# Output stage of a recurrent attention and maxout FFN kernel: x blocks taken into the Strassen products, and the first group's outputs in the same form

## The chip, the cores and the metric

One core of one Trainium2 chip. The metric is the device time of one execution in microseconds (us). Engines: TensorE (PE, with its weight loads as PEld), VectorE (DVE), ScalarE (ACT), GpSimd (POOL), and SyncE (SP), which here only issues DMAs.

## What is computed

```
batch, n_heads, seq, head_dim = 4, 8, 768, 48          # attention, float32
f = 1 / (1 + exp(-f_logit))
for t in range(seq):
    state = f[t][:, None] * state + outer(k[t], v[t])  # per batch and head, 48 x 48
    y[t] = q[t] @ state
x = y as (3072 tokens, 384)                            # 8 heads of 48 side by side
h = max(x @ w1, x @ w2, x @ w3)                        # 384 -> 768
out = h @ w_out                                        # 768 -> 384
```

## The kernel before

**Units and groups.** The recurrence is computed in chunks of 64 tokens. A unit `u` is one chunk of two batches (128 token rows); there are 24. Four units make a group of 512 tokens (`GRP`, `TOK`), so there are six groups. The attention of a unit is spread over the names `sigmoids`, `scan`, `after`, `before` (gates, keys `kh`, queries `qh`), `keys` and `keys_by_blocks` (keys turned back), `pairs` (line 392, with the causal mask on VectorE in line 395), `values` (lines 411 and 436), `carry` and `finish` (line 500).

**The FFN.** The maxout is taken as `x @ w1 + max(0, x @ (w2 - w1), x @ (w3 - w1))`. The linear part is folded into the output: `out = hm @ w_out + x @ (w1 @ w_out)`, with `hm` the maximum of 0 and the two differences. `linear` (line 745) makes `w1 @ w_out` once: `w_nat` has its rows in natural order, `w_lin` in the order in which later groups hold x (a copy by DMA, `place`). Group 0 has a form of its own, `ffn_first`; groups 1 to 5 make `hm` with `inputs_by_pairs` (line 836), itself a Strassen form, and the outputs with `outputs_by_pairs` (line 609).

**The output stage.** For groups 1 to 5 `hm @ w_out` is done as Strassen-Winograd: the 2x2 blocks are tiles of tokens (n), even and odd blocks of `hm` (k) and halves of the output columns. Seven products, each of three k blocks (`HJ`), 192 columns (`HD`) and two pairs of token tiles (p); `into(bank, p, lhs, rhs)` issues the three matmuls of one product and one pair. The sums of `hm` (s1, s2, s4, and one written in place) come from `sums_of_hm` on GpSimd, called in the last step `fourth(n)` of each third of `hm` after VectorE's two maximum operations (lines 886 and 887). The mixes of `w_out` come once from `mix` on GpSimd. The part `x @ (w1 @ w_out)` is four more products of three x blocks each, so a group takes 66 matmuls of 192 columns. They add into three PSUM banks a, b and c. Bank a is read three times on the way by ScalarE (`read`, line 614) and added to further after each read; VectorE and GpSimd form the output blocks from what was read (lines 617 and 662). In the last group the second half of c lies in b (`d`). Group 0's outputs are plain: `outputs` (line 563) takes, for each of four token tiles, six `hm` blocks and three x blocks of 384 columns: 36 matmuls.

**Order.** The whole kernel stands under a manual schedule: each engine and each DMA queue runs its instructions in the order of the program text. The FFN is a generator that yields the TensorE time of each step, counted as columns times 1.667 ns; the attention loop calls `fill(ns)`, which draws steps until the budget is used up. There are five draws per unit, of `EARLY` ns in units 4 to 7 (the last of the five 1000 less) and of `PART` ns afterwards; before unit 4 there are eight draws of 12,800 ns in all. So a step's place beside the attention follows from the sum of the draws and the sum of the yields. The FFN of a group runs while the units of the next group are computed; group 5's runs alone at the end, beside a check of the weights' range (`check_range`, ScalarE).

Of the kernel before, what the change touches and what calls it, by code (L numbers as in the profile page):

```python
# [9 lines left out]
FP32 = mybir.dt.float32  # L10
# [45 lines left out]
def kernel(  # L56
# [33 lines left out]
    def fast():  # L90
        ctx = ExitStack()
        with ctx:
# [434 lines left out]
            def bank(in_tr=False):  # L527
                if in_tr:
                    return ps_tr.tile([128, TOK], FP32, name="tr")
                return ps_f.tile([128, TOK], FP32, name="p")  # L530
# [26 lines left out]
            def outputs(hm, xT, i):  # L557
                p = bank()
                t = slice(i % 2 * UT, (i % 2 + 1) * UT)
                terms = [(hm[:, j, i * UT:(i + 1) * UT], w_out[:, j, :]) for j in range(NJ)]  # L560
                terms += [(by_halves(xT)[:, i // 2, k, t], w_nat[:, k, :]) for k in range(NK)]
                for n, (lhsT, rhs) in enumerate(terms):
                    nc.tensor.matmul(p[:, 0:DM], lhsT=lhsT, rhs=rhs, start=(n == 0), stop=(n == NJ + NK - 1))  # L563
                    if n % NK == NK - 1:
                        if n == NJ + NK - 1:
                            o = o_four[:, i]
                            nc.scalar.copy(o, p[:, 0:DM])
                            store(i, o)
                        yield NK * DM * COLUMN

            HJ, HD = NJ // 2, DM // 2
            corner = lambda k, n: w_out[:, k::2, n * HD:(n + 1) * HD]
            w_mix = [keep.tile([128, HJ, HD], FP32, name="mix")] + [w_in[2][:, :, n * HD:(n + 1) * HD] for n in range(4)]
            s_mix = [w_in[1][:, n, :].rearrange("q (jj t) -> q jj t", jj=HJ) for n in range(NK)]
            partial = [w_in[0][:, n, 0:DM] for n in range(NK)]
            pairs_of = lambda t: t.rearrange("q (p c) -> q p c", p=2)  # L580

            def mix(n):

                dst, x, y = ((w_mix[2], corner(1, 1), corner(0, 1)), (w_mix[0], corner(0, 1), corner(0, 0)),
                             (w_mix[1], corner(1, 1), w_mix[0]), (w_mix[3], corner(1, 0), w_mix[1]),
                             (w_mix[4], w_lin[:, :, 0:HD], w_lin[:, :, HD:]))[n]
                nc.gpsimd.tensor_tensor(dst, x, y, op=ALU.subtract)

            def sums_of_hm(hm, jj):

                first, second = ([hm[:, 2 * jj + k].rearrange("q (p n t) -> q n p t", p=2, n=2)[:, n] for n in range(2)]
                                 for k in range(2))
                s1, s2, s4 = (pairs_of(t[:, jj]) for t in s_mix)
                for dst, x, y, op in ((s1, first[1], second[1], ALU.add), (s2, s1, first[0], ALU.subtract),
                                      (first[1], first[0], first[1], ALU.subtract), (s4, second[0], s2, ALU.subtract)):
                    nc.gpsimd.tensor_tensor(dst, x, y, op=op)  # L596

            def outputs_by_pairs(g, hm, xT):
                tile_of = lambda p, n: slice((2 * p + n) * UT, (2 * p + n + 1) * UT)
                A = lambda k, n: lambda p: hm[:, k::2, tile_of(p, n)]  # L600
                X = lambda n: lambda p: xT[:, 0:NK, tile_of(p, n)]
                s1, s2, s4 = (lambda p, t=t: t[:, :, p * UT:(p + 1) * UT] for t in s_mix)
                lin = [w_lin[:, :, n * HD:(n + 1) * HD] for n in range(2)]
# [3 lines left out]
                def into(b, p, lhs, rhs):  # L607
                    for k in range(HJ):
                        nc.tensor.matmul(b[:, p * HD:(p + 1) * HD], lhsT=lhs(p)[:, k], rhs=rhs[:, k],  # L609
                                         start=id(b) not in begun, stop=(k == HJ - 1), skip_group_check=True)  # L610
                        begun.add(id(b))

                def read(b, n):
                    nc.scalar.copy(partial[n], b[:, 0:DM])  # L614
# [4 lines left out]
                COST = HJ * HD * COLUMN  # L619
                a, b, c = bank(), bank(True), bank(True)  # L620
                into(b, 0, X(0), lin[0])
                yield COST
                into(b, 1, X(0), lin[0])
                yield COST
                into(a, 0, A(0, 0), corner(0, 0))
                yield COST
                into(b, 0, A(1, 0), corner(1, 0))
                yield COST
                into(a, 1, A(0, 0), corner(0, 0))
                read(a, 0)  # L630
                yield COST
                into(b, 1, A(1, 0), corner(1, 0))
# [4 lines left out]
                into(a, 0, s2, w_mix[1])  # L637
                yield COST
                into(a, 1, s2, w_mix[1])
                read(a, 1)  # L640
                yield COST
                d = b if last else c
                into(c, 0, s1, w_mix[0])
# [4 lines left out]
                into(d, 1, s1, w_mix[0])  # L648
# [5 lines left out]
                into(a, 0, A(0, 1), w_mix[2])  # L654
                yield COST
                into(a, 1, A(0, 1), w_mix[2])
                yield COST
                into(a, 0, X(1), lin[1])
                yield COST
# [3 lines left out]
                if last:  # L663
                    store_part(g, 1, 1)
                yield COST
                into(c, 0, X(0), lin[1])
                yield COST
                into(d, 1, X(0), lin[1])
                yield COST
                into(a, 0, A(1, 1), w_mix[3])  # L670
                yield COST
                into(a, 1, A(1, 1), w_mix[3])
# [3 lines left out]
                into(a, 0, X(1), w_mix[4])  # L676
                yield COST
                into(a, 1, X(1), w_mix[4])
# [3 lines left out]
                yield COST  # L682
                into(c, 0, s4, corner(1, 1))
# [3 lines left out]
                into(d, 1, s4, corner(1, 1))  # L687
# [67 lines left out]
            def ffn_first(xT):  # L755
# [18 lines left out]
                for a in range(NK):  # L774
                    if a < 2:
                        for n in range(2 * NK + 2):
                            place(placed[a].bitcast(FP32), w_in[a + 1], n)
                    for cost in linear(a):
                        round_to(rounded[0] + 1)
                        yield cost  # L780
                for n in range(2 * NK + 2):
                    place(w_lin, w_nat, n)
                made = iter([lambda n=n: mix_in(n) for n in range(4)] + [lambda n=n: mix(n) for n in range(5)])
                for i in range(GRP):
                    for n, cost in enumerate(outputs(hm, xT, i)):
                        if i or n:
                            next(made, lambda: None)()
                        if i == GRP - 1 and n == 1 and 1 in packed:
                            sums_of_x(1)
                        yield cost  # L790
# [33 lines left out]
            def inputs_by_pairs(g, hm, xT):  # L824
# [57 lines left out]
                def fourth(n):  # L882
                    into(A[n], n, w_two[1][:, 1], t4)
                    yield COST
                    into(A[n], n, w_two[1][:, 2], t5)
                    nc.vector.scalar_tensor_tensor(out(n, 0), out(n, 0), 0.0, two(A[n]), op0=ALU.max, op1=ALU.max)
                    nc.vector.scalar_tensor_tensor(out(n, 1), out(n, 1), 0.0, u3, op0=ALU.max, op1=ALU.max)  # L887
                    sums_of_hm(hm, n)
                    yield COST
# [48 lines left out]
            EARLY = 2360  # L938
            PART = (33 * TOK + 22 * HJ * HD) * COLUMN / (5 * GRP)
# [408 lines left out]
```

## Time and profile before

| | us |
|---|---|
| median of 3 runs (423.09 to 423.75) | 423.5 |
| the profiled execution | 423.43 |
| its span, first to last instruction | 421.7 |
| group 0's outputs (98.3 to 127.1) | 28.7 |
| groups 1, 2 and 3, from one group's first FFN product to the next group's | 60.5 each |
| group 5's FFN to the last instruction (366.1 to 421.7) | 55.6 |

Times inside the profile count from the start of the span. A line of the timeline or of the chain has its start, its duration, the engine and the source line, and how many records were merged into it (`x6`); in brackets stands the idle time in front of it and what ended that. A matmul in float32 leaves two MATMUL and two weight load records. "p" and "tr" are the names of the PSUM tiles: bank a is a "p", banks b and c are "tr".

### The profile page before, as it was taken

The page shows a single profiled execution, that of the slowest core. Times are in us where ns is not written, and L with a number is a line of the kernel's source. Part 1 is how long each engine was busy: PE and PEld are TensorE (multiplying, and loading weights), DVE is VectorE, ACT ScalarE, POOL GpSimd, SP SyncE. Part 2 cuts the span into 40 slices and gives each one's busy share as a digit, 9 for nine tenths or more (in the row PEclk, how much of TensorE's full clock was granted, in tenths as well). Part 3 has the DMA queues.
Part 4 walks back from the last instruction along what each step waited for, and adds up shares of the span by engine and source line. Part 5 has one row for each costly group of instructions (what it writes and reads, how often), then busy time and mean ns, then how long its engine had stood idle before and what let it go on. Part 6 is the DMA issues. An engine that isn't in the chain of part 4 may idle for free.

```text
span 421.7 us, 11556 instructions
## 1 busy us (share of the span) xinstructions
PE 402.8 (96%) x4650; PEld 338.5 (80%) x4650; DVE 264.5 (63%) x515; ACT 180.2 (43%) x414; POOL 235.2 (56%) x262
## 2 busy tenths in 40 slices
PE   4978899899999999999999999999999999999995
PEld 3756765466668888998889988889988889988994
DVE  6986594843597699868789867889764730002300
ACT  2478676632114442425531444442254524576210
POOL 2189554621988676376586357576556960435600
PEclk9999999999999999999999999999999999999998
DMA  8999897782547654277645276635473010542002
GB/s 169 232 266 284 236 258 112 121 170 67 102 85 129 87 116 66 60 106 101 117 104 95 56 113 87 144 79 89 64 144 91 11 54 9 158 140 75 2 19 60
DMA packets 175129, 47.20 MB, mean 112 GB/s; under 512 B 154016, under 2 KB 172768, under 8 KB 175072
## 3 DMA queue, kind: packets, MB, share of 16 engines
q1 hardware_dynamic: 171600, 45.61, 52.0%
q10 hardware_dynamic: 3472, 0.81, 0.9%
q8 instruction: 37, 0.61, 0.6%
q14 instruction: 20, 0.16, 0.1%
HBM read 37.75 MB, written 4.72 MB: 101 GB/s over the span
## 4 chain that ended last, share of the span: by engine, by line
PE 86%; SPq 5%; DVE 3%; POOL 2%; issue 1%; ACT 1%; DMA 1%; DVEq 0%; POOLq 0%
PE p L836 19%; PE tr L836 16%; PE p L609 15%; PE tr L609 12%; PE p L563 6%; PE p L537 5%; PE p L745 3%; PE y L500 3%; PE y L411 3%; SPq L164 2%; PE a L392 2%; SPq L174 2%; PE y L436 2%; POOL w_in L258 1%; DMA placed<-in_moe_w_dram 1%
## 5 line engine op out<-in xcount | busy, mean ns | idle before, releaser
L836 PE MATMUL tr<-xT,placed 128*128 128x256 f32 x300 | 73.3, 385 | 0.0
L382 DVE STREAM_TRANSPOSE ks<-kh 32x128 f32<-32x128 f32 x224 | 67.7, 302 | 4.6 <-POOL kh L340 1.0
L836 PEld LDWEIGHTS tr<-xT,placed 128*128 128x128 f32 x300 | 55.6, 190 | 9.1 <-ACT hm L844 1.4
L836 PE MATMUL p<-xT,placed 128*128 128x256 f32 x180 | 45.0, 381 | 0.0
L537 PE MATMUL p<-xT,w_in 128*128 128x256 f32 (+1 forms) x108 | 34.4, 459 | 4.9 <-DVE hm L767 2.2
L836 PEld LDWEIGHTS p<-xT,placed 128*128 128x128 f32 x180 | 33.8, 190 | 4.7
L329 DVE TENSOR_TENSOR_SCAN r<-gate,from_one 128x520 f32<-128x520 f32 x24 | 31.3, 1306 | 8.9 <-ACT gate L308 5.9
L617 DVE TENSOR_TENSOR o<-tr,w_in 128x384 f32<-128x384 f32 (+1 forms) x11 | 5.7, 515 | 48.8 <-PE tr L609 43.5
L340 POOL TENSOR_TENSOR kh<-kt,r 128x512 f32<-128x512 f32 x16 | 28.7, 1796 | 10.6 <-DVE kt L296 10.6
L596 POOL TENSOR_TENSOR w_in<-hm 128x256 f32<-128x256 f32 x15 | 10.9, 727 | 40.5 <-DVE hm L887 40.5
L854 POOL TENSOR_TENSOR hm<-hm,rest_bits 128x512 f32<-128x512 f32 x15 | 22.7, 1514 | 19.2 <-ACT hm L844 19.2
L506 ACT COPY xT<-y 64x256 f32<-64x256 f32 (+1 forms) x60 | 22.1, 369 | 24.1 <-PE y L500 23.4
L347 DVE TENSOR_TENSOR_SCAN prod<-gate,from_inv 128x520 f32<-128x520 f32 x24 | 31.9, 1329 | 0.0
L395 DVE TENSOR_TENSOR at<-a,mask 128x512 f32<-128x512 f32 x24 | 16.5, 688 | 24.2 <-PE a L392 23.9
L836 PE MATMUL p<-w_in,placed 128*128 128x256 f32 x120 | 30.0, 379 | 0.0
L537 PEld LDWEIGHTS p<-xT,w_in 128*128 128x128 f32 x108 | 19.3, 190 | 13.0 <-issue 6.2
L258 POOL TENSOR_TENSOR w_in<-top_bits,rest_bits 128x384 uint32<-128x384 uint32 x18 | 21.8, 1218 | 13.5 <-DVE top_bits L254 8.0
L879 DVE TENSOR_TENSOR hm<-tr,hm 128x512 f32<-128x512 f32 x15 | 10.2, 681 | 29.3 <-PE tr L836 19.3
L662 POOL TENSOR_TENSOR o<-top_bits,w_in 128x384 f32<-128x384 f32 x5 | 5.1, 1018 | 41.6 <-ACT w_in L614 41.6
L614 ACT COPY w_in<-p 128x384 f32<-128x384 f32 x15 | 7.2, 480 | 47.3 <-PE p L609 47.3
L280 ACT ACTIVATE raw<-top_bits 128x384 f32<-128x384 f32 x48 | 25.3, 526 | 0.4
L836 PEld LDWEIGHTS p<-w_in,placed 128*128 128x128 f32 x120 | 22.8, 190 | 3.1
(155 smaller groups left out, 888.4 us busy)
## 6 DMA issues: line engine op xcount, KB each, us to landing
raw<-in_moe_w_dram SPq DMA_DIRECT2D x24, 384.0 KB, 4.2
v_ld<-in_v_dram SPq DMA_DIRECT2D x48, 96.0 KB, 3.3
placed<-in_moe_w_dram SPq DMA_DIRECT2D x12, 384.0 KB, 5.7
out_dram<-o SPq DMA_DIRECT2D x46, 96.0 KB, 2.2
placed<-in_moe_w_out_dram SPq DMA_DIRECT2D x6, 384.0 KB, 5.9
raw<-in_moe_w_out_dram SPq DMA_DIRECT2D x6, 384.0 KB, 3.3
f_ld<-in_f_logit_dram SPq DMA_DIRECT2D x32, 64.0 KB, 2.6
k_ld<-in_k_dram SPq DMA_DIRECT2D x32, 64.0 KB, 2.5
```

The lines of the kernel that those rows point to most:

```text
L258: nc.gpsimd.tensor_tensor(dst, by(top), by(rest), op=ALU.add)
L280: nc.scalar.activation(over, size, AF.Relu, scale=(-1 / HI_MIN, 1.0)[step - 1], bias=(1.0, -HI_END * (1 - 2.0 ** -24))[step - 1], accum_ou ...
L329: nc.vector.tensor_tensor_scan(r[:, 0:LEN][:, ::-1], flat(gate)[:, ::-1], flat(from_one)[:, ::-1], 1.0, op0=ALU.mult, op1=ALU.max)
L340: (nc.vector if u < BY_ROWS else nc.gpsimd).tensor_tensor(kh.rearrange("p h a t -> p a h t"), kt, by_batch(r[:, 1:LEN + 1].rearrange("p (x ...
L347: nc.vector.tensor_tensor_scan(flat(prod), flat(gate_tiles[u % 2]), flat(from_inv[u % 2]), 1.0, op0=ALU.mult, op1=ALU.max)
L382: nc.vector.transpose(ks[n * 32:(n + 1) * 32, :, par, e0:e0 + 32], kh[p0:p0 + 32, :, a, t0:t0 + 32])
L506: nc.scalar.copy(xT[o, :, t0 + a * C:t0 + (a + 1) * C], y[i, a, 0:HP * C].rearrange("p (h t) -> p h t", h=HP))
L537: nc.tensor.matmul(p if w < TOK else p.rearrange("p (two t) -> p two t", two=2), lhsT=w_in[i][:, kt, j * 128:(j + 1) * 128], rhs=x[:, t.st ...
L563: nc.tensor.matmul(p[:, 0:DM], lhsT=lhsT, rhs=rhs, start=(n == 0), stop=(n == NJ + NK - 1))
L609: nc.tensor.matmul(b[:, p * HD:(p + 1) * HD], lhsT=lhs(p)[:, k], rhs=rhs[:, k], start=id(b) not in begun, stop=(k == HJ - 1), skip_group_c ...
L836: nc.tensor.matmul(b[:, j * HALF:(j + 1) * HALF], lhsT=w[:, (2 * n + j) * 128:(2 * n + j + 1) * 128], rhs=x, start=begin and j == 0, stop= ...
L854: nc.gpsimd.tensor_tensor(out(n, 0), out(n, 0), first, op=ALU.add)
```

## The change

Groups 1 to 5: the x blocks 0 and 1 with the matching rows of `w_lin` become a fourth k block of the seven Strassen products (`mixed`), and only x block 2 stays in the four plain products. A group then takes 7·4·2 + 4·1·2 = 64 matmuls of 192 columns. The sums of x come from `sums_of_pair` on VectorE, two of the four operations in `fourth(1)` and two in `fourth(2)`; the mixes of `w_lin` come once, in group 1, from `mix_x` on VectorE.

Group 0 takes `outputs_by_pairs` too, without the mixed block: 66 matmuls of 192 columns. Its `hm` sums come from GpSimd during `linear`, and `mix` moves from GpSimd to VectorE, all five ahead of the first product.

In the order of the products, the s1 products come before the s2 products. `EARLY` goes from 2360 to 2270, and `PART` from 2464 to 2432 by its formula.

```
-            def outputs(hm, xT, i):
...
-            w_mix = [keep.tile([128, HJ, HD], FP32, name="mix")] + [w_in[2][:, :, n * HD:(n + 1) * HD] for n in range(4)]
+            w_mix = [corner(0, 1)] + [w_in[2][:, :, n * HD:(n + 1) * HD] for n in range(4)]
+            x_mix = [w_lin[:, 0, HD:]] + [w_mix[4][:, n] for n in range(2)] + [keep.tile([128, HD], FP32, name="mix")]
...
             def mix(n):
...
-                             (w_mix[4], w_lin[:, :, 0:HD], w_lin[:, :, HD:]))[n]
-                nc.gpsimd.tensor_tensor(dst, x, y, op=ALU.subtract)
+                             (w_mix[4], w_nat[:, :, 0:HD], w_nat[:, :, HD:]))[n]
+                nc.vector.tensor_tensor(dst, x, y, op=ALU.subtract)
+
+            def mix_x(n):
+                of = lambda k, c: w_lin[:, k, c * HD:(c + 1) * HD]
+                dst, x, y = ((x_mix[2], of(1, 1), of(0, 1)), (x_mix[0], of(0, 1), of(0, 0)),
+                             (x_mix[1], of(1, 1), x_mix[0]), (x_mix[3], of(1, 0), x_mix[1]),
+                             (w_mix[4][:, 2], of(2, 0), of(2, 1)))[n]
+                nc.vector.tensor_tensor(dst, x, y, op=ALU.subtract)
+
+            def sums_of_pair(x0, x1, *sums, part=slice(0, 4), engine=nc.gpsimd):
+                first, second = ([x.rearrange("q (p n t) -> q n p t", p=2, n=2)[:, n] for n in range(2)] for x in (x0, x1))
+                s1, s2, s4 = (pairs_of(t) for t in sums)
+                for dst, x, y, op in ((s1, first[1], second[1], ALU.add), (s2, s1, first[0], ALU.subtract),
+                                      (first[1], first[0], first[1], ALU.subtract), (s4, second[0], s2, ALU.subtract))[part]:
+                    engine.tensor_tensor(dst, x, y, op=op)
...
+                A = lambda k, n: lambda p: [hm[:, 2 * jj + k, tile_of(p, n)] for jj in range(HJ)] + [xT[:, k, tile_of(p, n)]] * mixed
...
+                if mixed:
+                    X = lambda n: lambda p: [xT[:, 2, tile_of(p, n)]]
...
+                    X = lambda n: lambda p: [by_halves(xT)[:, p, k, n * UT:(n + 1) * UT] for k in range(NK)]
...
-                into(a, 0, s2, w_mix[1])
-                yield COST
-                into(a, 1, s2, w_mix[1])
-                read(a, 1)
-                yield COST
                 d = b if last else c
-                into(c, 0, s1, w_mix[0])
+                into(c, 0, s1, T(0))
...
-                into(a, 0, A(0, 1), w_mix[2])
+                into(a, 0, s2, T(1))
                 yield COST
-                into(a, 1, A(0, 1), w_mix[2])
+                into(a, 1, s2, T(1))
+                read(a, 1)
+                yield COST
+                into(a, 0, A(0, 1), T(2))
+                yield COST
+                into(a, 1, A(0, 1), T(2))
...
-                    for cost in linear(a):
+                    for n, cost in enumerate(linear(a)):
                         round_to(rounded[0] + 1)
+                        if a and n < 2:
+                            jj = 2 * (a - 1) + n
+                            if jj < HJ:
+                                sums_of_hm(hm, jj)
                         yield cost
                 for n in range(2 * NK + 2):
                     place(w_lin, w_nat, n)
-                made = iter([lambda n=n: mix_in(n) for n in range(4)] + [lambda n=n: mix(n) for n in range(5)])
-                for i in range(GRP):
-                    for n, cost in enumerate(outputs(hm, xT, i)):
...
+                for n in range(5):
+                    mix(n)
+                for n, cost in enumerate(outputs_by_pairs(0, hm, xT)):
+                    if 3 <= n < 7:
+                        mix_in(n - 3)
+                    yield cost
...
                     sums_of_hm(hm, n)
+                    if n:
+                        sums_of_pair(xT[:, 0], xT[:, 1], *s_of_x(xT), part=slice(2 * n - 2, 2 * n), engine=nc.vector)
+                    if g == 1:
+                        for i in range(3 * n, min(3 * n + 3, 5)):
+                            mix_x(i)
...
-            EARLY = 2360
-            PART = (33 * TOK + 22 * HJ * HD) * COLUMN / (5 * GRP)
+            EARLY = 2270
+            PART = (33 * TOK + 64 * HD) * COLUMN / (5 * GRP)
```

## The prediction

> **What bounds the kernel now.** I read the page first, its busy times and the chain that ended last:
>
> ```profile
> PE 402.8 (96%) x4650; PEld 338.5 (80%) x4650; DVE 264.5 (63%) x515; ACT 180.2 (43%) x414; POOL 235.2 (56%) x262
> PE 86%; SPq 5%; DVE 3%; POOL 2%; issue 1%; ACT 1%; DMA 1%; DVEq 0%; POOLq 0%
> ```
>
> TensorE is the bound, so columns taken off it are worth their full time, and so is every wait put on it. The chain in order of time gives the pace, since its pieces are laid end to end. First four products of 384 columns, then the start of group 1's output stage (a product is two MATMUL records):
>
> ```profile
> 87.15 2.58 PE p L745 x8
> ...
> 160.03 1.93 PE p L836 x8
> 161.96 1.95 PE tr L609 x12
> 163.91 1.23 PE p L609 x6
> 165.13 0.97 PE tr L609 x6
> ```
>
> A 384-column product takes 2.58/4 = 0.645 us, a 192-column one 1.95/6 = 0.325: the same per column. Three products on line 609 take 0.97; the first three that read `hm` took 1.23. Why, the timeline of VectorE and of TensorE's weight loads in that place shows:
>
> ```profile
> 159.08 0.69 DVE L879 TENSOR_TENSOR hm<-tr,hm 128x512 f32<-128x512 f32 x1 [0.72 <-PE tr L836]
> 159.78 1.26 DVE L382 STREAM_TRANSPOSE ks<-kh 32x128 f32<-32x128 f32 x4
> 161.07 0.69 DVE L395 TENSOR_TENSOR at<-a,mask 128x512 f32<-128x512 f32 x1
> 161.68 0.70 DVE L296 STREAM_TRANSPOSE gate<-sig 128x512 f32<-128x512 f32 x1
> 162.41 1.24 DVE L329 TENSOR_TENSOR_SCAN r<-gate,from_one 128x520 f32<-128x520 f32 x1
> 163.69 0.21 DVE L332 RECIPROCAL from_inv<-r 128x8 f32<-128x8 f32 x1
> 163.81 0.68 DVE L886 SCALAR_TENSOR_TENSOR hm<-hm,p 128x512 f32<-128x512 f32 x1
> ...
> 164.54 0.30 PEld L609 LDWEIGHTS p<-w_out,hm 128*128 128x128 f32 x2 [0.28 <-DVE hm L886]
> ```
>
> The last maxout of the group (L886) is issued behind unit 11's mask and unit 12's scan, without a gap since 159.08. It ends at 164.49 and the weight load of `hm` block 4 starts at 164.54, 0.28 late. The chain shows 1.23 at this point in groups 1, 2 and 3, and 0.97 in groups 4 and 5, where no scan is left. So the cover in front of that load is already used up.
>
> Last, what a read of a bank costs that the next product adds into (group 5, no attention left), in the chain and in ScalarE's timeline:
>
> ```profile
> 368.69 0.86 PE p L836 x4
> 369.55 2.72 PE tr L836 x12
> ```
>
> ```profile
> 368.78 0.59 ACT L844 COPY hm<-tr 128x512 f32<-128x512 f32 x1 [0.74 <-PE tr L836]
> ```
>
> The bank's last product ended at 368.69; 0.86 of other products hid part of the copy, and the six after it took 2.72 for 2.59. The turn is 0.86 + 0.13 = 0.99 us with a copy of 0.59, so 0.40 lies around it; with the 384-column copy of L614 (0.48) I take 0.88.
>
> **The change part by part.** The sum is made on the profiled execution: 423.43 us, a span of 421.7 and 1.7 around it; the median of the runs is 423.5. A measurement tells apart about 0.2%, 0.85 us.
>
> *TensorE work.* Group 0's 36 products of 384 columns (23.2 us) become 66 of 192 (21.45): -1.8. Groups 1 to 5 go from 66 to 64 products: -0.65 each, -3.25. Together -5.0, all on the path.
>
> *The cover of the last maxout.* The stage still begins with X(0)·lin[0] twice, but with one block of x instead of three: 0.65 us instead of 1.95, then two `hm` blocks that are ready (0.65), then block 4. Does the attention stay in the same place? PART is chosen so that twenty draws equal one group in both versions (29,568 columns before, 29,184 after, times 1.667 ns), so the phase repeats. Adding draws and yields by hand: at unit 11's first draw 93.11 us have been drawn and 93.65 yielded, up to `third(2)`; the second draw brings both steps of `fourth(2)` and X(0)·lin[0], as the trace shows it today. So L886 stays behind the mask and the scan, and is not earlier. The load is wanted 1.30 sooner: the wait grows from 0.28 to 1.58 in groups 1, 2 and 3: +3.9. In groups 4 and 5 L886 starts right after TensorE (group 5: product end 394.73, L886 394.86 to 395.55); block 4 is wanted at 396.03, no wait.
>
> *Order of s1 and s2.* Before, `read(a, 1)` was followed by the s1 products, which do not touch bank a; after, A(0, 1) adds into a straight away. Full turn, 0.88, in groups 0 and 5. In groups 1 to 3 unit 12's finish and pairs (0.59 + 0.47) fall just between, by the same count of draws: 0. In group 4 only finish(23) does: 0.3. Together +2.05. What this order spares, the wait of s2 on `read(a, 0)`, cost nothing (0.97 of cover; no gap in the chain).
>
> *`read(a, 2)`.* X(0)·lin[1] twice stands between it and A(1, 1): 0.65 instead of 1.95, so 0.88 - 0.65 = 0.23 shows, in groups 1 to 5: +1.15. Group 0 keeps 1.95. Group 0 pays once at its start: its third x block reads `w_nat[2]`, just copied by L749 (0.48), with 0.65 of cover: +0.25.
>
> *New VectorE work.* A 128x256 operation with `hm` takes 0.412 (L767), a 192 one 0.358 (L617); back to back the next starts 0.08 earlier (L886 to L887: 0.60 for 0.68), so 0.33 and 0.28. Two sums of x stand behind L887 of `fourth(1)` ahead of the chain above: 0.66 against 0.72 idle there, about 0 in groups 2 and 3. In group 1 `mix_x` adds three (0.84) after `fourth(0)` against 0.45 idle, and two (0.56) after `fourth(1)`: with 0.66 - 0.72 some 0.9 that moves L886 and so the wait: +0.9. The other two sums come behind L887 and delay unit 12's kt by 0.7; its kh waited on GpSimd's sums anyway, and its mask has 1.16 idle in front: nothing. In group 4 and 5 VectorE idles: nothing.
>
> *Mixes moved.* In group 0 five mixes of 576 columns sit on VectorE behind unit 6's L444 (94.97). The first waits for the DMAs that read `w_in[2]` (GpSimd saw them land at 95.8), the second for the last L745 product (98.33). Queued behind: unit 7's mask, then scan 8. At 0.74 (0.358 for 192, 0.55 for 384, on to 576) four of them end at about 101.4; unit 7's pairs end near 101, and TensorE wants the mask only at 105. Nothing; if each took twice that, they end at 104.4, still before it. GpSimd gets twelve sums of `hm` (some 9.5 us) in a stretch where it waits (5.44 idle before 95.81); s1 wants them near 107. SP issues the same copies and group 0's stores later in one go, as it does for every other group: nothing.
>
> *EARLY.* 90 ns less per draw shifts steps against attention in units 4 to 6. TensorE waits there 0.6, 0.9 and 0.6 us (before 65.04, 74.64 and 82.25). The middle one is a bank held by L767 behind scan 6; with the second product of block 4 now behind unit 5's pairs, it should shrink. I take -0.5, between -2.1 (all go) and +1.5 (as much again).
>
> Sum: -5.0 + 3.9 + 2.05 + 1.15 + 0.25 + 0.9 - 0.5 = +2.75. 423.43 + 2.75 = 426.2, and with the median's 0.07 more, 426.3 us.
>
> On VectorE beside GpSimd the trace has rows: the mix L587 took 1.40 four times, and 2.21 beside scan 9, which itself took 1.37 instead of 1.24; L887 took 0.85 beside GpSimd's L357 and 0.68 otherwise. The bound for the new sums is so 0.33 to 0.5 each, up to 0.35 more in each of groups 1 to 3. [...]
>
> **The rivals.** *The column saving survives* (faster). If VectorE reaches L886 some 1.3 us earlier than today, or the steps of `fourth(2)` come out ahead of unit 11's pairs, the 3.9 and 0.9 fall away: 423.43 + 2.75 - 4.8 = 421.4; with EARLY's best 419.8, with its worst 423.4. It decides in favour if L886 starts within about 1.3 us after the last L836 product. For it: groups 4 and 5 do just that. Against it: 159.08 to 164.49 holds no idle time, and the order is fixed by the draws.
>
> *VectorE becomes the bound* (slower still). In 144 to 155 of the trace it has no gap; with some 3 us more in group 1 (four sums, five `mix_x`) and contention, delays would reach pairs and masks, another 1 us in each of groups 1 to 3: 429.3. Against it: masks and qh have 1 to 3 us to spare (unit 12's qh ends at 171.5, its pairs start at 174.6).
>
> *The waits mostly cancel* (no change): half of the 3.9 hidden gives 423.43 + 2.75 - 1.95 = 424.2, and with EARLY at its best 422.6. Nothing in the trace offers the second 0.65 of cover per group that this needs.
>
> **How the numbers follow.** Forecast 0.70, bounds from 426.3 - 1.6 (EARLY) to 426.3 + 2 + 1 (EARLY, contention): 424.7 to 429.3. Saving survives 0.14, cancel 0.06, VectorE bound 0.10. Faster 0.15, same 0.05, slower 0.80. To hold 8 in 10 I leave out most of the faster rival and the end of the VectorE one: 422.8 to 429.3.
>
> **What would show it.** Right: line 609's first three `hm` products in groups 1 to 3 cost some 2.3 to 2.6 us with L886 as their releaser; 0.9 of idle before A(0, 1) in groups 0 and 5 with L614's copy ending there; 0.2 before A(1, 1); group periods near 61.5 instead of 60.5. Wrong: L886 early with no wait behind it, or TensorE waiting on qh, `at` or the sums.

## The result, and the profile after

The changed kernel takes 441.92 us (median; 441.39 to 443.5) against 423.5: a ratio of 1.0442, 95% interval 1.0414 to 1.047. The profiled execution took 441.9, its span 440.2, 18.5 longer than before. Source lines moved: 609 is now 617, 836 is 846, 886 and 887 are 896 and 897, 879 is 889, 614 is 622, 745 is 753; the sums of `hm` and of x are line 586.

The page of the changed kernel, busy times and chain:

```profile
PE 407.0 (92%) x4690; PEld 349.1 (79%) x4690; DVE 286.1 (65%) x547; ACT 180.2 (41%) x415; POOL 240.2 (55%) x270
PE 79%; DVE 11%; ACT 3%; issue 2%; POOL 1%; DMA 1%; ACTq 0%; DVEq 0%; SPq 0%; POOLq 0%
```

TensorE was given less to do and is busy 4.2 us longer; VectorE's share of the chain went from 3% to 11%. So two things happened: TensorE waits on VectorE, and it runs slower. What TensorE waited for, by line (total, number, longest):

```profile
PE p L617 <- DVE hm L896: 9.4, 3, 4.2
...
PE p L753 <- POOL w_out L258: 2.0, 1, 2.0
...
PE y L436 <- DVE ks L382: 1.3, 2, 1.0
PE p L617 <- ACT w_in L622: 1.1, 2, 0.6
```

The first line is the last maxout of groups 1, 2 and 3. VectorE in front of it, group 2:

```profile
226.62 1.06 DVE L897 SCALAR_TENSOR_TENSOR hm<-hm,top_bits 128x512 f32<-128x512 f32 x1
227.60 1.91 DVE L586 TENSOR_TENSOR xT<-xT 128x256 f32<-128x256 f32 x2
229.53 1.25 DVE L382 STREAM_TRANSPOSE ks<-kh 32x128 f32<-32x128 f32 x4
230.79 0.69 DVE L889 TENSOR_TENSOR hm<-tr,hm 128x512 f32<-128x512 f32 x1
...
234.13 1.24 DVE L329 TENSOR_TENSOR_SCAN r<-gate,from_one 128x520 f32<-128x520 f32 x1
235.40 0.21 DVE L332 RECIPROCAL from_inv<-r 128x8 f32<-128x8 f32 x1
235.52 0.68 DVE L896 SCALAR_TENSOR_TENSOR hm<-hm,p 128x512 f32<-128x512 f32 x1
...
236.72 0.42 DVE L586 TENSOR_TENSOR xT<-xT 128x256 f32<-128x256 f32 x1
237.05 0.94 DVE L586 TENSOR_TENSOR s_last<-xT 128x256 f32<-128x256 f32 x1
```

There is no gap from 226.62 on. The two sums of x take 1.91 us (1.05 and 0.83), while GpSimd works on `state` and `hm`; the one at 236.72, with GpSimd idle until 236.94, takes 0.42. TensorE at the same place, and the granted clock behind the wait (windows of 1 us: span, busy of each engine, then PEclk):

```profile
232.83 0.81 PE L617 MATMUL p<-w_out,hm 128*128 128x192 f32 x4
236.25 0.91 PE L617 MATMUL p<-w_out,hm 128*128 128x192 f32 x2 [2.61 <-DVE hm L896]
```

```profile
236.00:237.00 1.00, 0.75 (x3) 0.75 (x4) 1.00 (x3) 0.00 (x0) 0.06 (x1) 0.69 0.76 95
237.00:238.00 1.00, 1.00 (x5) 1.00 (x4) 1.00 (x2) 0.00 (x0) 0.92 (x2) 0.50 0.76 102
238.00:239.00 1.00, 1.00 (x5) 1.00 (x4) 0.93 (x4) 0.00 (x0) 1.00 (x2) 0.50 0.57 96
239.00:240.00 1.00, 1.00 (x5) 0.85 (x3) 0.97 (x3) 0.00 (x0) 1.00 (x3) 0.60 0.61 105
```

After the wait TensorE runs at half clock for 3.4 us: 0.31 + 0.50 + 0.50 + 0.40 = 1.7 us lost. The same stands behind the longest wait of groups 1 and 3, and in group 0 behind this one:

```profile
89.09 1.17 PE L753 MATMUL p<-w_out,w_in 128*128 128x384 f32 x2 [1.97 <-POOL w_out L258]
```

Four times 1.7 is 6.8 us. By groups (us, from one group's first FFN product to the next; group 0 from the start of the span):

| | 0 | 1 | 2 | 3 | 4 | 5 |
|---|---|---|---|---|---|---|
| length before | 126.9 | 60.4 | 60.5 | 60.5 | 57.6 | 55.8 |
| TensorE busy | 113.2 | 60.4 | 60.5 | 60.5 | 57.6 | 50.6 |
| length after | 129.4 | 67.6 | 64.6 | 64.5 | 57.8 | 56.3 |
| TensorE busy | 113.2 | 62.1 | 62.0 | 61.9 | 57.3 | 50.5 |

Length less busy is idle time: it grew by 2.4 + 5.5 + 2.6 + 2.6 + 0.5 + 0.6 = 14.2. The busy time grew by 4.2, of which 6.8 is the slow clock, so the work itself shrank by 2.6. 14.2 + 6.8 - 2.6 = 18.4.

### The profile page after: what moved, and what is told of

It is laid out like the page before. It is cut to its first block, busy times and chain, and to the rows that moved or that the text cites. A ratio compares the mean times of both kernels' runs of the same rounds, so it can differ in the third digit from the quotient of the medians.

```text
span 440.2 us, 11678 instructions
## 1 busy us (share of the span) xinstructions
PE 407.0 (92%) x4690; PEld 349.1 (79%) x4690; DVE 286.1 (65%) x547; ACT 180.2 (41%) x415; POOL 240.2 (55%) x270
## 4 chain that ended last, share of the span: by engine, by line
PE 79%; DVE 11%; ACT 3%; issue 2%; POOL 1%; DMA 1%; ACTq 0%; DVEq 0%; SPq 0%; POOLq 0%
PE p L846 16%; PE p L617 16%; PE tr L846 15%; PE tr L617 12%; PE p L537 6%; DVE r L329 3%; PE y L411 3%; PE p L753 3%; PE y L500 2%; PE y L436 2%; PE a L392 2%; DVE ks L382 1%; ACT xT L506 1%; PE tr L291 1%; POOL w_in L258 1%
## 5 line engine op out<-in xcount | busy, mean ns | idle before, releaser
L340 POOL TENSOR_TENSOR kh<-kt,r 128x512 f32<-128x512 f32 x16 | 32.1, 2007 | 19.9 <-DVE kt L296 19.8
L339 POOL COPY ends<-r 128x8 f32<-128x8 f32 x24 | 6.6, 276 | 55.1 <-DVE r L329 52.4
L586 POOL TENSOR_TENSOR w_in<-hm 128x256 f32<-128x256 f32 x18 | 15.0, 836 | 39.0 <-DVE hm L897 39.0
L864 POOL TENSOR_TENSOR hm<-hm,rest_bits 128x512 f32<-128x512 f32 x15 | 22.0, 1466 | 16.6 <-ACT hm L854 16.6
L617 PE MATMUL p<-w_in,hm 128*128 128x192 f32 x144 | 29.0, 338 | 1.7 <-ACT w_in L622 1.1
L347 DVE TENSOR_TENSOR_SCAN prod<-gate,from_inv 128x520 f32<-128x520 f32 x24 | 30.2, 1260 | 0.0
L258 POOL TENSOR_TENSOR w_in<-top_bits,rest_bits 128x384 uint32<-128x384 uint32 x18 | 21.8, 1218 | 13.1 <-DVE top_bits L254 8.1
L617 PE MATMUL p<-w_in,xT 128*128 128x192 f32 x124 | 27.3, 336 | 0.0
L617 PE MATMUL tr<-w_out,w_in 128*128 128x192 f32 x144 | 27.0, 326 | 0.0
```

Of the source, the lines that this page charges most:

```text
L258: nc.gpsimd.tensor_tensor(dst, by(top), by(rest), op=ALU.add)
L340: (nc.vector if u < BY_ROWS else nc.gpsimd).tensor_tensor(kh.rearrange("p h a t -> p a h t"), kt, by_batch(r[:, 1:LEN + 1].rearrange("p (x ...
L347: nc.vector.tensor_tensor_scan(flat(prod), flat(gate_tiles[u % 2]), flat(from_inv[u % 2]), 1.0, op0=ALU.mult, op1=ALU.max)
L586: engine.tensor_tensor(dst, x, y, op=op)
L617: nc.tensor.matmul(b[:, p * HD:(p + 1) * HD], lhsT=x, rhs=w, start=id(b) not in begun, stop=(n == len(rhs) - 1), skip_group_check=True)
L864: nc.gpsimd.tensor_tensor(out(n, 0), out(n, 0), first, op=ALU.add)
```

## The experiments

All times are medians of two to eight runs; the kernel before, run beside them, had 423.3 to 424.4. Lengths of groups 0 to 5 in the profiled execution (the part of group 0 ahead of 65 us differs between the profiles by up to 1.7 us, whatever the edit; in e18, whose granted clock is 0.994 over the span for 0.999 in e17, and 1.00 from 75 to 419 us, that part is 2.5 longer than before):

| | us | ratio to before | 0 | 1 | 2 | 3 | 4 | 5 |
|---|---|---|---|---|---|---|---|---|
| e1_scan_late | 444.73 | 1.0484 (1.0393 to 1.0574) | 129.3 | 70.0 | 65.6 | 65.5 | 57.8 | 56.3 |
| e2_sums_behind | 444.09 | 1.0469 (1.0399 to 1.0538) | 130.1 | 66.5 | 65.5 | 65.4 | 57.8 | 58.1 |
| e3_warm | 438.7 | 1.0342 (1.03 to 1.0383) | 130.0 | 66.5 | 63.4 | 63.3 | 57.8 | 56.3 |
| e4_early_2360 | 441.16 | 1.0399 (1.0362 to 1.0437) | 127.4 | 68.4 | 64.5 | 64.5 | 58.7 | 56.1 |
| e5_gpsimd | 432.87 | 1.0193 (1.0109 to 1.0277) | 129.7 | 62.0 | 62.6 | 62.6 | 57.8 | 56.4 |
| e6_gpsimd_2360 | 437.68 | 1.0306 (1.0221 to 1.0392) | 126.6 | 67.1 | 62.8 | 64.4 | 58.7 | 56.1 |
| e7_before_dead | 428.47 | 1.0104 (1.008 to 1.0128) | 126.6 | 62.0 | 62.1 | 62.1 | 57.6 | 56.1 |
| e8_gpsimd_2360_s2 | 430.97 | 1.0148 (1.0065 to 1.0232) | 125.2 | 65.2 | 62.0 | 63.6 | 57.9 | 55.3 |
| e9_sums_early | 423.11 | 1.0001 (0.9984 to 1.0018) | 124.8 | 61.9 | 60.7 | 60.7 | 57.9 | 55.3 |
| e10_before_s1_first | 427.23 | 1.0089 (1.006 to 1.0117) | 126.8 | 61.3 | 61.3 | 61.3 | 58.4 | 56.6 |
| e11_before_2270 | 429.67 | 1.0144 (1.0073 to 1.0214) | 131.4 | 61.8 | 61.8 | 61.8 | 56.4 | 55.7 |
| e12_s2_first | 439.55 | 1.0377 (1.0337 to 1.0417) | 127.0 | 68.4 | 64.6 | 64.5 | 57.8 | 55.5 |
| e13_2360_s2_dve | 433.88 | 1.0218 (1.0144 to 1.0292) | 125.3 | 68.9 | 62.0 | 63.7 | 57.9 | 55.3 |
| e14_early_dve | 438.33 | 1.0323 (1.0252 to 1.0394) | 125.4 | 66.6 | 65.4 | 65.4 | 57.9 | 55.3 |
| e9_at_2400 | 424.79 | 1.002 (1.0002 to 1.0038) | 126.8 | 60.7 | 60.8 | 60.7 | 58.9 | 55.3 |
| e9_at_2440 | 425.42 | 1.0041 (1.0021 to 1.0061) | 126.6 | 60.8 | 60.6 | 60.5 | 58.9 | 55.3 |
| e17_group0_only | 421.2 | 0.9925 (0.99 to 0.995) | 125.9 | 60.2 | 60.2 | 60.2 | 57.7 | 55.8 |
| e18_group0_and_5 | 421.25 | 0.9932 (0.9906 to 0.9958) | 127.8 | 60.2 | 60.2 | 60.2 | 57.7 | 55.3 |

### Moving the wait: the first theory falls

The first theory was that the last maxout is late because of its place behind the scan on VectorE. Three edits of the changed kernel move things in that order; one fills the wait with spare products into a bank that is overwritten afterwards.

e1_scan_late puts units 12, 16 and 20's scan behind the maxout:

```
-                        scan(n)
+                        if u < 2 * GRP or u % GRP != 3:
+                            scan(n)
...
+                    if u >= 2 * GRP and u % GRP == 3 and n < NU:
+                        scan(n)
```

> The changed kernel, but in units 11, 15 and 19 the next unit's scan (with its gate transpose and reciprocal) is issued on VectorE after the last maxout of the group instead of in front of it. Theory A (the output stage waits for that maxout, which is queued behind the scan, and a wait of over 2 us also halves the granted clock for some 3 us after it): the wait in front of hm block 4 falls from 2.6 to about 0.6 us in groups 2 and 3 and from 4.2 to about 2 in group 1, the clock stays at 1.00 in groups 2 and 3; 430 to 434 us. Rival B (the loss lies in VectorE's load as a whole, so whatever is moved back returns as another wait): 439 to 442 us.

e2_sums_behind makes all four sums of x behind the last maxout (`if n == 2:` and no `part`).

> The changed kernel, but all four sums of x are issued behind the last maxout, none between the second and third maxout. Theory A with contention (the two early sums took 0.95 us each beside GpSimd instead of 0.42 and push the mask, the scan and the last maxout back by 1.4 us): the wait in groups 2 and 3 falls from 2.6 to about 1.2 us, without the clock's drop; in group 1 from 4.2 to about 2.5; 432 to 435 us. If only the lost cover counts (1.3 us) and the sums' place does not matter: 441 to 443 us.

e3_warm, in `outputs_by_pairs` ahead of the products that wait:

```
+                for _ in range({1: 10, 2: 6, 3: 6}.get(g, 0)):
+                    nc.tensor.matmul(a[:, 0:256], lhsT=ident, rhs=from_one..., start=True, stop=True)
```

> The changed kernel with dummy products of 256 columns (ten in group 1, six in groups 2 and 3, 0.43 us each) ahead of the output stage's first hm product, into the bank that this product then starts anew; they fill the wait and nothing else. If the halved clock after the wait costs time by itself (1.5 to 1.7 us in each of three groups): granted clock 1.00 after the wait, 436 to 438 us. If the clock's drop costs nothing, because TensorE would wait for something else then: 441 to 443 us.

e4_early_2360 sets `EARLY` back to 2360, with which `fourth(2)` comes ahead of unit 11's pairs.

> The changed kernel with EARLY at 2360 as before. By the count of draws and yields both steps of fourth(2) then come ahead of unit 11's, 15's and 19's pairs, mask and scan, and two steps of linear ahead of unit 6's. Theory A: no wait for the last maxout in groups 1 to 3, no halved clock; the wait for GpSimd's w_out rounding near 88 us goes back from 2.0 to 0.6; read(a, 1) now shows its full 0.9 us in every group; 424 to 427 us. Rival B (VectorE's load): 436 to 442 us.

Neither e1 nor e2 helped: the changed kernel's 1.0442 lies in both intervals, and both times lie above both of their ranges. e4 came out 0.8 us lower, in the range of its rival B. In e1 the wait on L896 fell from 9.4 to 3.1 us, and in its place stood 8.6 us of a new one; e4 shows the same trade:

```profile
PE y L436 <- DVE ks L382: 8.6, 8, 2.1
...
PE p L617 <- DVE hm L896: 3.1, 3, 2.1
```

```profile
PE y L436 <- DVE ks L382: 7.4, 8, 2.0
...
PE p L617 <- DVE hm L896: 0.7, 1, 0.7
```

(e1 above, e4 below.) Whatever is taken out from in front of the maxout lands in front of the blocks of keys (`ks`) that the next product of the attention needs. e3 shows what the slow clock is worth: with the wait filled, no slice of groups 1 to 3 shows the slow clock and each is 1.0 to 1.2 us shorter, although the spare products take as long as the wait. In group 2 the output stage with them takes 1.7 less, and the next products of the attention (L436), which now wait for `ks`, take 0.5 more. That led to theory C of the next expectations: VectorE's queue between `third(2)` and those keys has no room left.

### The engine and the place of the sums

e5_gpsimd, and e6_gpsimd_2360 with `EARLY = 2360` besides:

```
             def mix_x(n):
...
-                nc.vector.tensor_tensor(dst, x, y, op=ALU.subtract)
+                nc.gpsimd.tensor_tensor(dst, x, y, op=ALU.subtract)
...
-                        sums_of_pair(xT[:, 0], xT[:, 1], *s_of_x(xT), part=slice(2 * n - 2, 2 * n), engine=nc.vector)
+                        sums_of_pair(xT[:, 0], xT[:, 1], *s_of_x(xT), part=slice(2 * n - 2, 2 * n))
```

> The changed kernel with the x sums of fourth(1) and fourth(2) and the subtractions of mix_x on GpSimd instead of VectorE; nothing else. Theory C (VectorE's in-order queue from third(2) to the next group's ks is full, and what the change put on it, plus the lost cover, becomes a wait of TensorE that also halves the clock): the wait on hm L896 falls from 2.61 to about 1.6 us, no slice of groups 2 and 3 shows a clock of 0.50, their periods are 61 to 61.5 us instead of 64.5, the time 429 to 432 us. Rival (the added blocks and their order cost the time, whatever engine makes the sums): 438 to 442. Second rival (GpSimd, not VectorE, becomes late: s2 and s1 wait for L586 on GpSimd): the waits move to s1 products of the output stage, 434 to 440.

> As e5_gpsimd with EARLY back at 2360, the value of the kernel before. Theory C: with VectorE's queue as short as before, the earlier fourth(2) leaves no wait on hm L896 and no new one on ks L382, the wait on w_out L258 in group 0 is back at 0.6 us with no halved clock behind it: 424 to 427 us. Rival (the wait only moves, as it did in e4_early_2360): 434 to 441.

e7_before_dead, in `fourth(n)` of the kernel before:

```
+                    for h in range(2 if n else 0):
+                        nc.vector.tensor_tensor(xT[:, NK, 0:HALF], xT[:, 0, 0:HALF], xT[:, 1, 0:HALF], op=ALU.add)
```

> The kernel before, with two dead sums of 128x256 (xT by halves, into a part of xT that nothing reads by then) on VectorE after the maxout of fourth(1) and of fourth(2): VectorE's load of the changed kernel without its products, order or EARLY. Groups 2 and 3 of the kernel before do not run any of their first products on it. Theory C: the two sums ahead of the last maxout take 1.4 to 1.9 us and make the wait on hm L886 1.6 instead of 0.28, and the two behind it come in front of ks: 1.3 to 3 us in each of groups 1 to 3, the time 428 to 432. Rival (VectorE has room; only the lost cover of the changed kernel counts): 423.5 to 425.

e8_gpsimd_2360_s2 is e6 with the s2 products moved back ahead of s1.

> As e6_gpsimd_2360 with the s2 products ahead of the s1 products again, so that the read of a behind s2 is covered by s1 and A(0,1) does not wait for it. Theory C: another 1 to 3 us off e6_gpsimd_2360 (0.6 to 1.2 per group in groups 0 to 5 for the wait on ACT L622, and the last maxout covered as in the kernel before): 420 to 424. Rival (the order of s1 and s2 matters only for s2's own wait on hm): within 0.7 of e6_gpsimd_2360.

e5 took 9.1 us off; the wait on L896 was 6.2 in all, 1.60 in group 1 as expected but 2.29 in groups 2 and 3, and no slow clock followed it in group 2 (1.00 from 191.7 to 254.2). The scan in front of the maxout is what made it longer; in group 2:

```profile
227.52 2.25 DVE L329 TENSOR_TENSOR_SCAN r<-gate,from_one 128x520 f32<-128x520 f32 x1
229.80 0.21 DVE L332 RECIPROCAL from_inv<-r 128x8 f32<-128x8 f32 x1
...
230.65 0.30 PEld L617 LDWEIGHTS p<-w_out,hm 128*128 128x128 f32 x2 [2.59 <-DVE hm L896]
```

The two sums of x had moved GpSimd's add of line 882 to 227.40, beside the scan, which took 2.25 us and not 1.24. The weight load waited 2.59: 0.28 as before, 1.30 of lost cover, and these 1.01.

e7 is the cleanest of the four: VectorE's load alone, in a kernel that is otherwise the old one, costs 4.7 us, 1.6 in each of groups 1 to 3. The time is theory C's; the wait on L886 is not, with 0.47 in group 2 for an expected 1.6, and 0.16 and 0.34 on `ks`. e6 fell in the range of its rival and e8 missed both: the wait moved to `ks` again although VectorE had less to do. VectorE's timeline in e8 says why:

```profile
226.25 0.69 DVE L897 SCALAR_TENSOR_TENSOR hm<-hm,top_bits 128x512 f32<-128x512 f32 x1 [1.32 <-POOL top_bits L882]
```

VectorE stood still for the add to `u3`, which on GpSimd was now queued behind the first two sums of x. So e9_sums_early puts all four sums behind that add, and `mix_x` behind `join` in group 1, where GpSimd was idle:

```
                     nc.gpsimd.tensor_tensor(u3, u3, U5[n], op=ALU.add)
+                    if n == NJ // 2 - 1:
+                        sums_of_pair(xT[:, 0], xT[:, 1], *s_of_x(xT))
```

> As e8_gpsimd_2360_s2, with the GpSimd work put where GpSimd was idle in the kernel before: the four x sums right behind the add to u3 in seventh(2) (not in fourth(1) and fourth(2), where the first pair stood ahead of that add, so that VectorE waited 1.32 us in groups 2 and 3 and 2.90 in group 1 for it), and the mix_x subtractions behind join(0) and join(1) of group 1. Theory C, now with GpSimd's queue as the link to VectorE's: the wait on top_bits L882 goes, and with it the wait on ks L382 (1.38 in groups 2 and 3, 2.2 in group 1): 1.3 to 1.7 us less in groups 2 and 3 each, 3 to 5 less in group 1: 421 to 425 us. Rival (the ks come late for VectorE's own length): 428 to 431.

It came out at 423.11. With the engine as the only difference to e9:

```
-                        sums_of_pair(xT[:, 0], xT[:, 1], *s_of_x(xT))
+                        sums_of_pair(xT[:, 0], xT[:, 1], *s_of_x(xT), engine=nc.vector)
```

> As e9_sums_early with the four x sums on VectorE in the same place of the program (behind the u3 add of seventh(2)), mix_x still on GpSimd: only the engine differs. Theory C (VectorE's queue is full there): the ks L382 of unit 11, 15 and 19 come 1.7 to 3.8 us later (four sums at 0.42 to 0.95 us), so a wait of 1.5 to 3 us in each of groups 1 to 3, and where it passes 1.8 us a halved clock: 428 to 434. Rival (the place did it, not the engine): 422.5 to 424.5.

It cost 15.2 us, more than expected: 4.7 in each of groups 1 to 3. Group 2 in e9 on GpSimd (above) and in e14 on VectorE (below):

```profile
221.02 2.56 POOL L586 TENSOR_TENSOR xT<-xT 128x256 f32<-128x256 f32 x3
223.53 0.73 POOL L586 TENSOR_TENSOR s_last<-xT 128x256 f32<-128x256 f32 x1
```

```profile
223.23 2.46 DVE L586 TENSOR_TENSOR xT<-xT 128x256 f32<-128x256 f32 x3
225.61 1.49 DVE L586 TENSOR_TENSOR s_last<-xT 128x256 f32<-128x256 f32 x1
```

The sums are no quicker on VectorE (3.9 us for four, with GpSimd busy beside them) than on GpSimd (3.2). On GpSimd they fall into idle time; on VectorE they become two waits, 1.50 on L901 (the maxout) and 1.41 on `ks`, with 0.34 more in the keys, and one slow stretch of 1.7: 4.95, less the 0.35 that e9 waits for `ks` too is 4.6, against 4.7 measured.

### The order of s1 and s2, and EARLY

e10_before_s1_first moves the block of the s2 products behind that of s1 in the kernel before; e12_s2_first moves it back in the changed kernel; e11_before_2270 has only `EARLY = 2270` in the kernel before; e13_2360_s2_dve is e12 with `EARLY = 2360`.

> The kernel before with the s1 products ahead of the s2 products in the output Strassen scheme, as in the changed kernel, and nothing else. My prediction's terms for it: the last maxout loses its cover in groups 1 to 3 (the wait on hm L886 from 0.28 to 1.58 us each, 3.9) and A(0,1) waits for the read of a behind s2 (0.88 in group 5, 0.3 in group 4): 428 to 429. Rival (what the lost cover costs is small without the x sums, as s2's own operands come later than s1's): 423.5 to 425. Second rival (the wait also halves the clock): 430 to 433.

> The kernel before with EARLY 2270 instead of 2360 and nothing else. By e4_early_2360 (group 0 ends 2.0 us earlier at 2360, groups 1 to 3 0.1 to 0.8 later) and the prediction's bounds (minus 2.1 to plus 1.5): 423 to 426 us if the wait on w_out L258 in group 0 grows to 1.97 us here too and halves the clock behind it. Rival (w_out L258 is late only because of the changed kernel's mixes): 421.5 to 423.5.

> The changed kernel (x sums on VectorE, EARLY 2270) with the s2 products ahead of s1 again, and nothing else. Theory C: the cover of 1.3 us returns and A(0,1) does not wait, and with waits below 1.8 us no clock is lost: the wait on hm L896 falls from 2.61 to about 1.3 in groups 2 and 3 and to about 3 in group 1, the time 432 to 435 us. Rival (the x sums, not the order, make the wait; s2's operands come as late): 438 to 442.

> The changed kernel with EARLY 2360 and s2 ahead of s1, both as before, so that only the mixed blocks and VectorE's sums are left of the change. If the parts add up: e9_sums_early's 423.1 plus the 4.8 that e7_before_dead showed for the sums on VectorE, plus 1 to 2 for mix_x in group 1: 428 to 431 us. If they don't (theory C with the clock: the wait passes 1.8 us and halves the clock behind it): 433 to 439, with a wait on ks L382 of about 2 us and slices at 0.50 in each of groups 1 to 3.

e10 came near its number by another way: no wait on L886 grew (0.28 in the weight loads, as before), and all of the 4 us is A(0, 1) waiting in each of groups 1 to 5 for the copy of bank a; the weight load of that product in group 2:

```profile
235.02 0.95 PEld L609 LDWEIGHTS p<-w_in,hm 128*128 128x128 f32 x6 [0.86 <-ACT w_in L614]
```

The expectation had put the lost cover down to the order. It isn't: that cover is the width of the x products ahead of block 4 (the prediction had it so), which e10 leaves alone. e12 says the same from the other side, in the range of its rival: with s2 first the wait on L896 in groups 2 and 3 is still 2.60.

e11 is the surprise. 90 ns per draw cost 6.4 us in a kernel whose sums and products were untouched: in group 0 the same wait on `w_out` L258 (1.96) with the same slow clock behind it, and 1.3 more in each of groups 1 to 3, where `third(2)` and so the last maxout now stand behind unit 12's scan on VectorE (group 2: L332 ends at 227.4, L879 starts at 227.33):

```profile
PE p L609 <- DVE hm L886: 4.0, 3, 1.4
...
PE p L745 <- POOL w_out L258: 2.0, 1, 2.0
```

The mixes, which the rival blamed, are not in that kernel. The 1.3 per group is not among the changed kernel's losses: there `third(2)` (L889, 230.79) stands ahead of the scan (234.13), as in the kernel before. e13 fell where the parts don't add up: 11.7 us of span over e9, 7.0 of them in group 1, where `mix_x` comes on top and two stretches are slow. Group 3 has one slow stretch, group 2 none, and so they differ by 1.7.

e9 at other values of `EARLY`:

> e9_sums_early with EARLY 2400. By a hand count of draws it moves X0l0 of group 1 ahead of unit 11's finish and puts unit 6's and 7's steps one product later. If the phase is a term of several us in either direction: outside 422 to 424.5; rival (e9_sums_early stands on a plateau): 422 to 424.5. No theory of mine gives its sign.

> e9_sums_early with EARLY 2440; as e9_at_2400, one product further in group 0 and in unit 12. Same two expectations: outside or inside 422 to 424.5 us.

Both lie just outside, by 0.3 and 0.9. Behind the product at 65 us group 0 takes 60.99 and 61.87 for 60.26 in e9; group 4 loses 1.1 and group 1 wins 1.2. So e9's place is no plateau, and there is no better one among these three.

### Where the mixed blocks pay

e9 is no faster than the kernel before, with group 0 2.1 us shorter. So the mixed blocks were taken out, and put back in group 5 alone:

```
-                mixed = g > 0
+                mixed = False                    # e17_group0_only
+                mixed = g == NU // GRP - 1       # e18_group0_and_5
```

(with the x parts, `PART` and one GpSimd subtraction for `w_mix[4]` to match.)

> e9_sums_early without the mixed blocks: groups 1 to 5 take the plain x products of the kernel before, with no x sums and no mix_x; of the change only group 0's outputs in Strassen form are left, with its mixes on VectorE, its sums of hm on GpSimd and one subtraction for the x part on GpSimd in group 1. By the periods of e9_sums_early's group 0 (2.1 us shorter) and of the kernel before in groups 1 to 5: 421.4 us. Rival (the shorter group 0 is given back in group 1, as in e9_sums_early, where it grew by 1.5): 422.8 to 423.5.

> As e17_group0_only, with the mixed blocks in group 5 alone (its x sums and mix_x on GpSimd there). By e9_sums_early's group 5 (0.6 us shorter than before): 0.6 below e17_group0_only, so 420.8 us. Rival (mix_x in group 5 or the sums come late there): the same as e17_group0_only or up to 1 us above it.

e17 takes 421.2 us, 0.75% below the kernel before, and the forecast was 421.4: this is the version that beats both. The split isn't quite the one forecast. From the product at 65 us on, group 0 takes 61.86 before and 60.27 in e17, 1.6 less and not 2.1; groups 1 to 3 are 0.3 shorter each, and the wait of 0.28 on the last maxout is gone there. e18 isn't told apart from e17: its group 5 is 0.5 shorter in the profile, its time the same.

Why the mixed blocks don't pay in groups 1 to 3 even with the sums on GpSimd, TensorE shows in group 2, in the kernel before (above) and in e9 (below):

```profile
227.06 0.63 PE L436 MATMUL y<-v_ld,ks 64*64 64x48 f32 x32
```

```profile
226.72 0.27 PE L436 MATMUL y<-v_ld,ks 64*64 64x48 f32 x4
227.15 0.31 PE L436 MATMUL y<-v_ld,ks 64*64 64x48 f32 x2
227.80 0.66 PE L436 MATMUL y<-v_ld,ks 64*64 64x48 f32 x26 [0.35 <-DVE ks L382]
```

In e9 these products wait for `ks` and take 1.74 us instead of 0.63, and 0.6 of the difference counts as busy; the output products of the group, from start to start, take 22.29 before and 21.68 in e9. So 0.6 is saved and 1.1 is lost.

## Why the prediction was wrong

The sign held; the sum of +2.75 was short by 16 us, and the time is far outside the range. By its own steps:

**New VectorE work: the step that failed first.** The sums of x were priced at 0.33 and `mix_x` at 0.28, and "about 0 in groups 2 and 3". They took 1.05 and 0.83 in front of the maxout, and `mix_x` 0.35 where GpSimd was idle at its start and 0.77 to 0.89 otherwise. With these sizes the prediction's own sum works: 1.3 of lost cover, plus 1.91 for the sums and 0.2 for the longer L897, less 0.72 of idle, is 2.7 against 2.61 measured in groups 2 and 3; in group 1, with 1.77 for two `mix_x`, 4.5 against 4.21. The mechanism was right, the duration was off by three times, and the upper bound (0.5) lay below it. The rows that the price came from, L767 and L617, have one of their two inputs in PSUM (`p`, `tr`), so they are not of the kind that was added: in the kernel before L767 took 0.42 beside GpSimd's L258 (31.39) and 0.41 alone (46.21), L617 0.54 beside L340 (169.54) and 0.56 alone (349.80), while in the changed kernel L897, with `hm` and `top_bits` as its inputs, took 0.68 alone (214.36) and 1.06 beside L864 and L357 (226.62). The rows that were at hand, L587 at 2.21 against 1.40 and L887 at 0.85 against 0.68, showed that such operations slow each other, not how far.

In the changed kernel a sum of x took 0.42 where GpSimd stood idle at its start, and 0.83 to 1.05 where it was at work.

**The clock: a cost that had no term.** 6.8 us, four stretches of 1.7. The trace of before has waits of up to 1.45 (at 29.79) and full clock from 9.1 to 418.7, so it gave no row for it.

**The other sums.** "Delays unit 12's kt by 0.7: nothing" was wrong in kind. The keys behind the second pair were as short of time as the maxout: e7 has a wait on `ks` of 0.16 and 0.34 in group 2, and e1, e4 and e13 turn most of the loss into it. The rival "VectorE becomes the bound" came nearest, at 0.10 and at too low a price; but the waits stood on the maxout and the keys, not on pairs and masks.

**EARLY.** Taken as -0.5 between -2.1 and +1.5. In group 0 it was -0.34 (the middle wait, 0.92 to 0.58, as forecast) + 1.97 (L258) + 1.7 (clock) = +3.3. In the profile of e4, the change with 2360, group 0 is 2.0 shorter; from the product at 65 us on, it takes 61.10 for 64.67, 3.6 shorter. The wait that grew was a fourth one, not among the three that the bound counted.

**The order of s1 and s2.** Priced at 0.88 in groups 0 and 5. Both waits are there (0.57 on TensorE, 0.86 in its weight loads), and e10 shows 0.86 where it bites. Right there; in group 4, priced at 0.3, the same wait stood (0.85). Right too is A(1, 1): its weight load waits 0.21 in group 2, priced at 0.23.

**The cover of the last maxout.** Right in cause and size: e5 shows it without the sums, as above. In its group 1 the weight load waits 1.90, which is 0.28 + 1.30 and 0.32 for a scan of 1.56 instead of 1.24.

**TensorE work.** -1.8 in group 0, with +0.25 at its start, held: from the product at 65 us on, group 0 is 1.60 shorter in e9. TensorE's busy time falls by 0.3 in groups 2 and 3 instead of 0.65, and by 0.6 and 0.5 in 4 and 5. In group 2 the output products did get 0.61 shorter; the wait for `ks` that is counted as busy hides it.

**The mixes in group 0.** The first took 1.07, the rest 0.75 to 0.76, near the price (0.74); they held up nobody.

How the +18.4 splits into causes is settled for group 0. From the product at 65 us on, it takes 61.86 before, 60.26 with its outputs in Strassen form (e9), 61.10 with s1 first as well (e4) and 64.67 with `EARLY` 2270 besides: -1.6 + 0.8 + 3.6. For groups 1 to 3 the split stays open. The parts measured alone in the kernel before (EARLY 6.4, order 4.0, two pairs of sums 4.7) do not add up to the whole with -2.6 for the columns, and need not: whether a slow stretch appears depends on how several waits lie together (in e8 group 3 has one and group 2 none, with the same two waits).

## What to carry to other kernels

An engine that is 63% busy may still have stretches with no room: before work is put on it, find the stretch where it goes in and count its idle time there, and price the work by rows of the same kind in which the neighbour, here GpSimd, is busy too (a sum of x took 0.42 and 1.05, L767 0.41 and 0.42). Look for where the engine with idle time has it, and put the work in that gap and not before something another engine waits for; here the same four sums cost 15 us more on the one engine than on the other. A term of a schedule that shifts everything by a little, such as EARLY, deserves a run by itself.

## What the runs showed of the hardware

**Half clock in stretches of 3.41 us.** The length of one wait does not decide. TensorE's granted clock fell to 0.50 behind 1.97, 2.61 and 4.21 us of waiting in the changed kernel; behind 2.29 in group 2 of e5 (1.00 from 191.7 to 254.2) and 1.96 in group 0 of e12 (1.00 from 75 to 153) it stayed at 1.00, and in e12's group 1 waits of 0.96 and 0.34 for `ks` were enough (0.50 from 153.00 on). The 2 us in the expectation of e1 and the 1.8 us in those of e12, e13 and e14 were the author's estimates; no run shows either as a limit.

What the traces have in common is a grid. In the changed kernel half clock begins at 89.61, 171.52, 236.38 and 301.23 and lasts 3.41 us each time; these starts are 24, 19 and 19 times 3.413 us apart. In e12 it begins at 153.00, 170.08, 234.92 and 299.78, which is 5, 19 and 19 times 3.413 us apart, and in e14 at 171.90, 236.76 and 301.60, 19 and 19 times. In the 3.41 us in front of its four starts in the changed kernel TensorE was busy for 1.45, 0.00, 0.80 and 0.81 us. In e8 groups 2 and 3 have the same waits of 1.38 and 0.34 for `ks`, but at another place in the grid; two stretches of group 2 and two of group 3:

```profile
231.05:234.46 3.41, 2.08 (x35) 1.91 (x36) 3.25 (x9) 0.00 (x0) 2.37 (x4) 1.00 0.42 51
234.46:237.87 3.41, 3.41 (x23) 3.41 (x22) 3.33 (x11) 0.38 (x2) 2.96 (x3) 1.00 0.65 169
292.49:295.90 3.41, 1.69 (x40) 1.40 (x33) 3.25 (x8) 0.43 (x2) 2.37 (x4) 1.00 0.76 91
295.90:299.31 3.41, 3.41 (x13) 3.41 (x12) 3.21 (x8) 0.00 (x0) 3.41 (x3) 0.50 0.75 175
```

Behind 2.08 us of work the next stretch has full clock, behind 1.69 half. In the changed kernel (11 to 400 us) and in e11 to e14 (75 to 400 us) half clock followed no stretch of the grid with more than 2.11 us of work (e12, from 149.59), and full clock none with less than 1.66 (e14, from 161.66); in between both occur, so the busy time in front does not settle it alone. This is read off the traces afterwards; no run was made to test it.

**VectorE beside GpSimd.** A 128x256 float32 sum of x took 0.42 when it started with GpSimd idle; when GpSimd was at work it took 0.83 to 1.05 in the changed kernel, and in e14 three took 2.46 together and the fourth 1.49. GpSimd's own sum of `hm` went from 0.73 to 0.90 in the changed kernel (228.33). VectorE's scan of line 329 went from 1.24 to 2.25 (e5). Not every row is slowed: in the kernel before the scan took 1.24 beside GpSimd's L854 (192.06), and L767 0.42 beside L258.
